# A hand-written order of 3920 steps is replaced by another, and two VectorE steps no longer wait for each other

## The chip, the cores and the metric

One core of a Trainium2 chip runs the program. The time is the device time of one execution in microseconds (us), the median of the runs; three runs of the kernel before took 1454.66 to 1455.35 us. Engines are named PE (TensorE), DVE (VectorE), ACT (ScalarE) and POOL (GpSimd) in the profile; SP issues transfers.

## What is computed

Three stages over 8192 tokens of 192 numbers, all in float32 from the outside:

```python
# 1: every token is a softmax-weighted sum of itself and the 6 tokens before it, 8 heads of 24
w = softmax(weight_gen, axis=-1)                      # (2, 4096, 8, 7)
out = einsum('bshk,bskhg->bshg', w, windows_of_7(x))  # x: (2, 4096, 192)
x = out.reshape(8192, 192)
# 2: a gated layer, 192 -> 1536 -> 192
x = (sigmoid(x @ w_gate) * (x @ w_val)) @ w_out
# 3: a rational layer, 192 -> 2048 -> 192
h = x @ w_in
P = a[0] + a[1]*h + a[2]*h**2 + a[3]*h**3
Q = 1 + abs(b[0])*abs(h) + abs(b[1])*h**2
return (P / (Q + 1e-6)) @ w_out2
```

## The kernel before

The tokens go through in blocks of 512 (the last two of 256), 17 in all. Matmuls of stages 1 and 2 run in a rounded float32 form; each operand is split into a high and a low part, so that a product takes five matmuls.

**The order.** Every piece of work is a *step* with a short name (`do_g`, `do_S`, ...). A step that is done hands the next one its data with `then`, into a queue of that name. The string ORDER (line 40) lists 3920 names, and `run(ORDER)` (line 713) calls them one after the other; each call takes the oldest work of its name. As every engine runs its instructions in the order in which they were issued, ORDER fixes the order on each engine and on each transfer queue. Semaphores do the rest: an instruction waits for its data and for its buffer. So what a step's place in ORDER decides is what stands before and behind it on its own engine.

**The steps**, by what they do for a block:
- Stage 1: X loads the next x (line 161), Na, Nb and Nc make the softmax weights, B multiplies a shifted x by one tap's weights on VectorE (line 397), J adds that product to the sum with an adding transfer that GpSimd issues (line 413). Six J belong to a block; after the last one Z copies the tail columns on ScalarE (line 422), T1 transposes on TensorE, C1 and L1 split the result into high and low.
- Stage 2, for each of 12 chunks: g and v are five matmuls each into the one PSUM bank `pg` and the one bank `pv`. S is the sigmoid on ScalarE (line 472), which frees `pg`; M multiplies on VectorE and frees `pv`; G rounds to the high part on ScalarE; L on VectorE or l on GpSimd subtracts for the low part (line 496: one function, two engines); O adds the chunk to the output with five matmuls. E, E1, E2, C2 and L2 split that output for stage 3.
- Stage 3, for each of 16 chunks: H is five matmuls into one of two banks `h` (line 555); A is three activations on ScalarE (line 562); V and W on VectorE finish the numerator's powers and free the bank. For each pair of chunks: Q adds the two parts of the denominator with an adding transfer that GpSimd issues (line 588), R takes the reciprocal square root on ScalarE, U squares it (line 598), T and Y multiply by it and D corrects it, all three on VectorE by way of the helper at line 585 (lines 603 to 615). P is a chunk's output matmuls, in full float32 (line 627); F copies the finished block out (line 636).
- The weights come in during the first blocks, by the steps K, Ka, Kd, Kh, Kl (VectorE) or kl (GpSimd), and Kc.

R and S use different activation tables of ScalarE, and Nb (exp) a third; a change from one to another puts a table load in between.

In the middle the list repeats itself every two blocks, and a pair of blocks has two stretches of the same kind: a last B, the J behind it, and Z, each followed by the S and g that come next.

Of the kernel before, what the change touches and what calls it, by code (L numbers as in the profile page):

```python
# [40 lines left out]
X K Na Z Na Ka T1 Kd C1 Ka L1 K Kh Ka kl g Ka Nb Kd v Nb Nc K Kh Ka Kl S B Nc B Kc Kd J B Kh K g Ka Kl S Kd Kc J B  # L41
Kh Kl K Kd g Ka Kd Kh Ka Kl J Kh K Kl B M Kd v G K S g B Kh l M v G S Kl K O Kd M l Kc v G Kh l O Kl J O K M G L g
Ka Kd v S Ka g O J Kc S B Kh Kl X Kd M g Kc G v S L J Kh g K Ka Kl M O Kd G v S Ka g Kd Z Kh T1 K l M C1 v L1 kl G O
S M g G B Kh v S l Kc Ka g Kl Ka B O K B M l v G S L J Ka g M Kd v S g K O M Kd S v G K Kh g O Kl K B G Kh L Ka l O
M Kc S v Kl J G Ka g Ka L M Kc O Kd S g G Ka v L Kh K O B M kl O G v S L J Kc g M Kd v G S Ka g O M l K S v G B E g
M l E1 v S Kh Kd g Ka E2 M kl K O C2 S L2 v G Kd g Kc L J O M H Kd G K S v L A g M J B v S V X Ka g W Kd Ka O Kd O K
G H G L l M O S J Kd g G A v L H M Q V S v A W O M Z V v G W Ka l T1 O M C1 L1 O G l g G B v S R L g M B H Na J U v
A T H Y O A Q D O G V E l W S V H W O B A M J g B v G V S l W R g M Q E1 v Kd G E2 H C2 U L J O L2 A T H Y P R D O A
V P W U Q V H S W P T A M g B v G V S l H W R M g J Y v G D A O L B H U Q V P S W T J O Nb M g Kd v G Nc A H P A l V
W P Y S Q H D O A V g W M H V G S W l v A g M B G v S V l X R g W J M O Q R v G H U L U P T A P Y D O R V H Z U W P  # L50
T A H Y Q O D A P V S W P V W g M T G v S R L g M Y T1 G v D O L C1 L1 P U B S H T H A M Y g G v D S A g V l W O Q M
S V g G W l H S B v A B J g M Q H V S W P A O V P G W E l v E1 R J E2 M g B C2 H R L2 O U v G T A H M l P U V J W S
P Q Y O F D g G T A H Y v S l V A g W D H R Q V P W M O A B P B J G V v U l W H R M T O A Y v G D H U V l P A W J T
P S Q V O W H Y g D A H M B G v S V l X A g W J M P S Q V R W g O P G U L v Z T H R M Y O U v D G A H T P l A V W P
Q Y S O D H V g W A M H Na G v V S l A W g M Q P S V R W O T1 G P B U L v T O C1 L1 P R M g Y G U H l v A D H T Q P
A V W O S V H W Y P A D g Q V H S W g M B G v S L J A g M B O S V P W G E L v E1 R E2 M J g B C2 H R L2 O U v G T A
H M l P U V J W S P Q Y O F D g G T A H Y v S l V A g W D H R Q V P W M O A B P B J G V v U l W H R M T O A Y v G D
H U V l P A W J T P S Q V O W H Y Nb g D A H Nc P A Q V O W R M P V W v B G H U L J X O T R H A Y P D A Q P V W P Z
V U W H S T H Y A g D P S M Q V G g A W l v O S M V G g W l v S R g M v G T1 R M l O U B v T O C1 L1 P G U l H S Y H
D A g M P T G S v A V l W g Q M V O S W g Y G H l S v A D g M V Q H S W P B A B J O V P G W E l v E1 R E2 M g C2 H B  # L60
J R O L2 U v G T A H M l P U V Q W S P J Y O F D g G T A H Y v S l V A g W D H R Q V P W M O A B P B J G V v U l W H
R M T O A Y v G D H U V l P A W J T P S Q V O W H Y g D A H M B G v S V l X A g W J M P S Q V R W g O P G U L v Z T
H R M Y O U v D G A H T P l A V W P Q Y S O D H V g W A M H Na G v V S l A W g M Q P S V R W O T1 G P B U L v T O C1
L1 P R M g Y G U H l v A D H T Q P A V W O S V H W Y P A D g Q V H S W g M B G v S L J A g M B O S V P W G E L v E1
R E2 M J g B C2 H R L2 O U v G T A H M l P U V J W S P Q Y O F D g G T A H Y v S l V A g W D H R Q V P W M O A B P B
J G V v U l W H R M T O A Y v G D H U V l P A W J T P S Q V O W H Y Nb g D A H Nc P A Q V O W R M P V W v B G H U L
J X O T R H A Y P D A Q P V W P Z V U W H S T H Y A g D P S M Q V G g A W l v O S M V G g W l v S R g M v G T1 R M l
O U B v T O C1 L1 P G U l H S Y H D A g M P T G S v A V l W g Q M V O S W g Y G H l S v A D g M V Q H S W P B A B J
O V P G W E l v E1 R E2 M g C2 H B J R O L2 U v G T A H M l P U V Q W S P J Y O F D g G T A H Y v S l V A g W D H R
Q V P W M O A B P B J G V v U l W H R M T O A Y v G D H U V l P A W J T P S Q V O W H Y g D A H M B G v S V l X A g  # L70
W J M P S Q V R W g O P G U L v Z T H R M Y O U v D G A H T P l A V W P Q Y S O D H V g W A M H Na G v V S l A W g M
Q P S V R W O T1 G P B U L v T O C1 L1 P R M g Y G U H l v A D H T Q P A V W O S V H W Y P A D g Q V H S W g M B G v
S L J A g M B O S V P W G E L v E1 R E2 M J g B C2 H R L2 O U v G T A H M l P U V J W S P Q Y O F D g G T A H Y v S
l V A g W D H R Q V P W M O A B P B J G V v U l W H R M T O A Y v G D H U V l P A W J T P S Q V O W H Y Nb g D A H
Nc P A Q V O W R M P V W v B G H U L J X O T R H A Y P D A Q P V W P Z V U W H S T H Y A g D P S M Q V G g A W l v O
S M V G g W l v S R g M v G T1 R M l O U B v T O C1 L1 P G U l H S Y H D A g M P T G S v A V l W g Q M V O S W g Y G
H l S v A D g M V Q H S W P B A B J O V P G W E l v E1 R E2 M g C2 H B J R O L2 U v G T A H M l P U V Q W S P J Y O
F D g G T A H Y v S l V A g W D H R Q V P W M O A B P B J G V v U l W H R M T O A Y v G D H U V l P A W J T P S Q V
O W H Y g D A H M B G v S V l X A g W J M P S Q V R W g O P G U L v Z T H R M Y O U v D G A H T P l A V W P Q Y S O
D H V g W A M H Na G v V S l A W g M Q P S V R W O T1 G P B U L v T O C1 L1 P R M g Y G U H l v A D H T Q P A V W O  # L80
S V H W Y P A D g Q V H S W g M B G v S L J A g M B O S V P W G E L v E1 R E2 M J g B C2 H R L2 O U v G T A H M l P
U V J W S P Q Y O F D g G T A H Y v S l V A g W D H R Q V P W M O A B P B J G V v U l W H R M T O A Y v G D H U V l
P A W J T P S Q V O W H Y Nb g D A H Nc P A Q V O W R M P V W v B G H U L J X O T R H A Y P D A Q P V W P Z V U W H
S T H Y A g D P S M Q V G g A W l v O S M V G g W l v S R g M v G T1 R M l O U B v T O C1 L1 P G U l H S Y H D A g M
P T G S v A V l W g Q M V O S W g Y G H l S v A D g M V Q H S W P B A B J O V P G W E l v E1 R E2 M g C2 H B J R O
L2 U v G T A H M l P U V Q W S P J Y O F D g G T A H Y v S l V A g W D H R Q V P W M O A B P B J G V v U l W H R M T
O A Y v G D H U V l P A W J T P S Q V O W H Y g D A H M B G v S V l X A g W J M P S Q V R W g O P G U L v Z T H R M
Y O U v D G A H T P l A V W P Q Y S O D H V g W A M H Na G v V S l A W g M Q P S V R W O T1 G P B U L v T O C1 L1 P
R M g Y G U H l v A D H T Q P A V W O S V H W Y P A D g Q V H S W g M B G v S L J A g M B O S V P W G E L v E1 R E2
M J g B C2 H R L2 O U v G T A H M l P U V J W S P Q Y O F D g G T A H Y v S l V A g W D H R Q V P W M O A B P B J G  # L90
V v U l W H R M T O A Y v G D H U V l P A W J T P S Q V O W H Y Nb g D A H Nc P A Q V O W R M P V W v B G H U L J X
O T R H A Y P D A Q P V W P Z V U W H S T H Y A g D P S M Q V G g A W l v O S M V G g W l v S R g M v G T1 R M l O U
B v T O C1 L1 P G U l H S Y H D A g M P T G S v A V l W g Q M V O S W g Y G H l S v A D g M V Q H S W P B A B J O V
P G W E l v E1 R E2 M g C2 H B J R O L2 U v G T A H M l P U V Q W S P J Y O F D g G T A H Y v S l V A g W D H R Q V
P W M O A B P B J G V v U l W H R M T O A Y v G D H U V l P A W J T P S Q V O W H Y g D A H M B G v S V l X A g W J
# [19 lines left out]
def tile_kernel(ctx: ExitStack, tc: tile.TileContext, x, wg, w_gate, w_val, w_out1, w_in, w_out2, ca, cb, out):  # L115
# [629 lines left out]
```

## Time and profile before

| | us |
|---|---|
| median of 3 runs | 1454.94 (1454.66 to 1455.35) |
| the profiled execution | 1458.93 |
| its span in the profile | 1457.2 |
| TensorE, VectorE, ScalarE, GpSimd busy | 1353.4, 1249.1, 1208.6, 436.3 |
| granted TensorE clock, mean | 0.98 |

The span is the profiled execution from its first to its last instruction. A granted clock of 1.00 is the full 2.4 GHz. Busy times are those in which an engine had an instruction running; a wait is idle time ahead of an instruction, put down to what ended it. Five of the pairs of blocks lie between the copies F that start at 261.08 and 1114.22 us.

### The profile page before, as it was taken

What the parts mean: (1) busy time and instruction counts of PE and PEld (TensorE: products, weight loads), DVE (VectorE), ACT (ScalarE), POOL (GpSimd) and SP (SyncE); (2) the same over time, 40 slices, a digit from 0 to 9 for tenths busy, and PEclk for the clock granted to TensorE, in tenths of its full rate; (3) what the DMA queues carried; (4) which work ended last, traced back from release to release, by engine and by line L of the source; (5) the groups of instructions that cost most, each with busy time, mean ns of one, the idle gap of its engine ahead of it and who ended that gap; (6) DMA issues with size and microseconds to landing.
All of it is one profiled execution on the core that took longest, in us unless ns stands there. A gap on an engine that the chain in (4) does not pass through costs nothing.

```text
span 1457.2 us, 18316 instructions
## 1 busy us (share of the span) xinstructions
PE 1353.4 (93%) x6630; PEld 1159.0 (80%) x6630; DVE 1249.1 (86%) x1547; ACT 1208.6 (83%) x1733; POOL 436.3 (30%) x394
## 2 busy tenths in 40 slices
PE   1589999999999999999899999999999999999877
PEld 0367788888888888888788888888888888999777
DVE  7888888889798897989889797989979788878987
ACT  2455898989898897989889898888988988889985
POOL 5223322423243232423234232432324333222110
PEclk9699999999999999999999999999999999999999
DMA  6776453534545353554525355453535434433442
GB/s 159 182 191 155 87 118 65 126 63 98 107 87 120 70 107 75 100 113 87 118 55 124 73 102 107 77 120 69 111 69 113 101 71 89 79 67 67 85 96 55
DMA packets 51227, 144.12 MB, mean 99 GB/s; under 512 B 6212, under 2 KB 16322, under 8 KB 51136
## 3 DMA queue, kind: packets, MB, share of 16 engines
q0 software_dynamic: 32256, 102.51, 37.9%
q1 hardware_dynamic: 18880, 40.44, 9.2%
q8 instruction: 52, 0.85, 0.2%
q14 instruction: 39, 0.32, 0.1%
HBM read 31.51 MB, written 6.29 MB: 26 GB/s over the span
## 4 chain that ended last, share of the span: by engine, by line
PE 43%; DVE 18%; ACT 14%; DMA 11%; issue 9%; POOL 4%; SPq 0%; POOLq 0%; DVEq 0%; ACTq 0%
PE acc L627 11%; DVE v L585 6%; DMA x<-pr 5%; DMA q<-r 4%; DVE v L576 3%; POOL gl L498 2%; ACT r L594 2%; DVE q L585 2%; DVE v L581 2%; PE h L292 2%; ACT r L599 2%; PE h L293 2%; PE pg L292 2%; PE h L296 2%; PE h L295 2%
## 5 line engine op out<-in xcount | busy, mean ns | idle before, releaser
L627 PE MATMUL acc<-wo,v 128*128 128x192 f32 x2048 | 375.2, 331 | 13.6 <-DVE v L585 13.6
L627 PEld LDWEIGHTS acc<-wo,v 128*128 128x128 f32 x2048 | 349.5, 194 | 30.7 <-DVE v L585 13.1
L498 POOL TENSOR_TENSOR gl<-g,gh 128x512 fp32r<-128x512 f32 x141 | 222.0, 1574 | 476.5 <-ACT gh L492 476.5
L567 ACT ACTIVATE v<-h,co 128x512 f32<-128x512 f32 x256 | 199.8, 780 | 49.0 <-PE h L296 48.4
L589 POOL DMA_DIRECT2D q<-r x128 | 118.6, 926 | 326.2 <-ACT r L569 280.3
L576 DVE TENSOR_TENSOR v<-v,h 128x512 f32<-128x512 f32 x256 | 174.7, 683 | 35.1 <-ACT r L569 34.1
L581 DVE SCALAR_TENSOR_TENSOR v<-v,co,h 128x512 f32<-128x512 f32 x256 | 191.5, 748 | 9.1
L585 DVE SCALAR_TENSOR_TENSOR q<-q,r 128x1024 f32<-128x1024 f32 x128 | 156.7, 1224 | 40.2 <-ACT r L599 40.2
L585 DVE SCALAR_TENSOR_TENSOR v<-v,co,r 128x1024 f32<-128x1024 f32 x128 | 180.8, 1413 | 0.0
L569 ACT ACTIVATE r<-h,co 128x512 f32<-128x512 f32 x256 | 178.3, 696 | 0.0
L486 DVE TENSOR_TENSOR g<-sg,pv 128x512 f32<-128x512 f32 x192 | 131.3, 684 | 53.5 <-PE pv L296 43.7
L568 ACT ACTIVATE q<-h,co 128x512 f32<-128x512 f32 x256 | 176.2, 688 | 0.4 <-DVE v L585 0.4
L585 DVE SCALAR_TENSOR_TENSOR v<-q,v 128x1024 f32<-128x1024 f32 x128 | 168.4, 1316 | 4.0
L594 ACT ACTIVATE r<-q,co 128x1024 f32<-128x1024 f32 x128 | 147.3, 1153 | 19.7 <-DMA q<-r 19.0
L492 ACT CAST gh<-g 128x512 fp32r<-128x512 f32 x192 | 118.6, 618 | 51.7 <-DVE g L486 38.2
L474 ACT ACTIVATE sg<-pg 128x512 f32<-128x512 f32 x192 | 115.6, 602 | 38.7 <-PE pg L296 29.6
L416 POOL DMA_DIRECT2D x<-pr x96 | 85.6, 892 | 171.8 <-DVE pr L280 94.8
L599 ACT ACTIVATE r<-r 128x1024 f32<-128x1024 f32 x128 | 135.5, 1062 | 0.3
L292 PE MATMUL h<-X2h,W0h 128*128 128x512 f32 (+1 forms) x272 | 111.0, 408 | 13.1 <-DVE v L581 12.8
L292 PE MATMUL pg<-X1h,W0h 128*128 128x512 f32 (+1 forms) x192 | 80.8, 421 | 26.6 <-ACT sg L474 26.6
L293 PE MATMUL h<-X2l,W0h 128*128 128x512 f32 (+1 forms) x272 | 103.2, 379 | 0.0
L295 PE MATMUL h<-X2h,WT 128*128 128x512 f32 (+1 forms) x272 | 102.9, 378 | 0.0
(135 smaller groups left out, 2819.0 us busy)
## 6 DMA issues: line engine op xcount, KB each, us to landing
q<-r POOLq DMA_DIRECT2D x128, 512.0 KB, 4.6
x<-pr POOLq DMA_DIRECT2D x84, 384.0 KB, 4.2
x<-in_x_dram SPq DMA_DIRECT2D x13, 960.0 KB, 5.8
out_dram<-o SPq DMA_DIRECT2D x15, 384.0 KB, 4.2
v<-in_moe_w_out_dram SPq DMA_DIRECT2D x14, 384.0 KB, 4.0
x<-in_x_dram SPq DMA_DIRECT2D x3, 768.0 KB, 4.7
WT<-r SPq DMA_DIRECT2D x36, 64.0 KB, 3.2
x<-pr POOLq DMA_DIRECT2D x12, 192.0 KB, 3.5
```

Of the source, the lines that this page charges most:

```text
L292: mm(d, W0h[:, w], h[:, 0, :], start=True, stop=False)
L293: mm(d, W0h[:, w], lo[:, 0, :], start=False, stop=False)
L498: eng.tensor_sub(gl, g1, gh.bitcast(F32))
L567: nc.scalar.activation(v[:, e, :], ph, AF.Identity, scale=a3, bias=a2)
L568: nc.scalar.activation(q[:, e, :], ph, AF.Square, scale=b1r)
L569: nc.scalar.activation(a[:, e, :], ph, AF.Abs, scale=b0)
L576: nc.vector.tensor_mul(v, v, ph)
L581: nc.vector.scalar_tensor_tensor(out=v, in0=v, scalar=a1, in1=ph, op0=ALU.add, op1=ALU.mult)
L585: nc.vector.scalar_tensor_tensor(out=out, in0=in0, scalar=scalar, in1=in1, op0=op0, op1=op1, reverse0=neg)
L594: nc.scalar.activation(r, q, AF.Abs_reciprocal_sqrt, scale=USC, bias=usb)
L599: nc.scalar.activation(r, r, AF.Square, scale=2.0 ** -20)
L627: mm(acc[:, s // 2, (s % 2) * D:(s % 2 + 1) * D], g[:, (e * jb + s) * P:(e * jb + s + 1) * P], wo2[:, c, :], start=(c == 0 and s % 2 == 0) ...
```

## The change

ORDER is replaced as a whole. Every step occurs as often as before, but for one kind of choice: of the 192 subtractions for the low part 96 run on VectorE (L) and 96 on GpSimd (l), where it was 51 and 141, and of the 16 subtractions for weights 15 run on VectorE (Kl) and one on GpSimd (kl), where it was 12 and 4. T and Y follow U independently now, and D follows when both are done. All functions but these stay as they are:

```diff
     @step
     def do_U(b, p, v, q, r):
         nc.scalar.activation(r, r, AF.Square, scale=2.0 ** -20)
-        then("T", b, p, v, q, r)
-
-    @step
-    def do_T(b, p, v, q, r):
+        then("T", b, p, v, q, r, both := [])
+        then("Y", b, p, v, q, r, both)
+
+    def second(both, *work):
+        both.append(1)
+        if len(both) == 2:
+            then(*work)
+
+    @step
+    def do_T(b, p, v, q, r, both):
         stt(q, q, EPS1, r, ALU.add, ALU.mult)
-        then("Y", b, p, v, q, r)
-
-    @step
-    def do_Y(b, p, v, q, r):
+        second(both, "D", b, p, v, q)
+
+    @step
+    def do_Y(b, p, v, q, r, both):
         stt(v, v, a0, r, ALU.add, ALU.mult)
-        then("D", b, p, v, q)
+        second(both, "D", b, p, v, q)
```

Of ORDER, the two stretches of a pair from the last B of a block to the g behind the next S (the first kind, then the second; the lists before and after go through the same work in different order, so the stretches do not match step by step):

```
before  B G H U L J X O T R H A Y P D A Q P V W P Z V U W H S T H Y A g
after   B P M J X R V g W H U O A Y v T H G R l V P W Z Q D A P O U V H W S Y H A M g
before  B G v S V l X A g W J M P S Q V R W g O P G U L v Z T H R M Y O U v D G A H T P l A V W P Q Y S O D H V g
after   B A P J X G V v R l W P M g U R H Y U O T v G D Z H A Na P L A Q V P W Y O S V H W g
```

## Rows read from the trace of the kernel before

**Rows 1.** The page's first part: busy time, share of the span, instructions of each engine.
```profile
PE 1353.4 (93%) x6630; PEld 1159.0 (80%) x6630; DVE 1249.1 (86%) x1547; ACT 1208.6 (83%) x1733; POOL 436.3 (30%) x394
```

**Rows 2.** Busy time by stretch: length; busy and count of each engine; granted clock, DMA share, GB/s.
```profile
26.50:160.00 133.50, 106.59 (x414) 80.18 (x415) 113.29 (x210) 75.04 (x147) 38.08 (x34) 0.90 0.65 166
...
261.08:1114.22 853.14, 830.15 (x3981) 711.63 (x3980) 735.45 (x856) 746.31 (x1041) 271.14 (x235) 0.99 0.47 95
...
1402.85:1457.20 54.35, 40.65 (x224) 38.10 (x222) 42.56 (x45) 35.03 (x48) 5.16 (x6) 0.87 0.35 73
```

**Rows 3.** TensorE's waits, 261 to 1114 us: total, times, longest.
```profile
PE pg L292 <- ACT sg L474: 16.2, 10, 3.6
PE h L292 <- DVE v L581: 6.8, 18, 0.8
```

**Rows 4.** ScalarE's waits for transfers in the same stretch.
```profile
ACT o L426 <- DMA x<-pr: 19.3, 10, 3.7
...
ACT r L594 <- DMA q<-r: 9.1, 7, 1.8
```

**Rows 5.** Timeline of ScalarE: start, length, instruction, idle time before it; Z and one R.
```profile
463.02 0.62 ACT L426 COPY o<-x 128x512 f32<-128x512 f32 x1 [0.92 <-DMA x<-pr]
465.49 1.15 ACT L594 ACTIVATE r<-q,co 128x1024 f32<-128x1024 f32 x1 [1.85 <-DMA q<-r]
...
723.99 0.62 ACT L426 COPY o<-x 128x512 f32<-128x512 f32 x1 [3.67 <-DMA x<-pr]
```

**Rows 6.** Timeline, 713 to 719 us: the last B, the x load, J and Q.
```profile
713.76 0.95 DVE L280 TENSOR_TENSOR pr<-x,wn 128x768 f32<-128x768 f32 x1
...
714.74 0.33 SPq L165 DMA_DIRECT2D x<-in_x_dram  x1
...
715.00 0.86 POOL L416 DMA_DIRECT2D x<-pr  x1 [3.98 <-DVE pr L280]
...
718.78 0.86 POOL L589 DMA_DIRECT2D q<-r  x1 [2.92 <-ACT r L569]
```

**Rows 7.** Timeline of TensorE, at 473 and from 722 us.
```profile
473.87 0.50 PE L292 MATMUL pg<-X1h,W0h 128*128 128x512 f32 x1 [0.81 <-ACT sg L474]
...
722.37 0.39 PE L296 MATMUL h<-X2l,WT 128*128 128x512 f32 x1
...
723.50 0.39 PE L296 MATMUL h<-X2l,WT 128*128 128x512 f32 x1
727.53 0.80 PE L292 MATMUL pg<-X1h,W0h 128*128 128x512 f32 x1 [3.64 <-ACT sg L474]
...
731.52 0.53 PE L292 MATMUL pg<-X1h,W0h 128*128 128x512 f32 x1
```

**Rows 8.** Busy time of one stretch, its granted clock third from the end.
```profile
727.50:731.00 3.50, 3.47 (x9) 2.99 (x10) 3.43 (x5) 2.73 (x5) 0.86 (x1) 0.51 0.00 0
```

**Rows 9.** The chain of waits at 268 us: start, length, the eight matmuls of one P.
```profile
268.52 1.30 PE acc L627 x8
```

**Rows 10.** Timeline of GpSimd at 457 us: a J and the Q behind it.
```profile
456.68 0.87 POOL L416 DMA_DIRECT2D x<-pr  x1
457.26 1.18 POOL L589 DMA_DIRECT2D q<-r  x1
```

**Rows 11.** Groups by line and form: busy us, mean ns; idle before.
```profile
L498 POOL TENSOR_TENSOR gl<-g,gh 128x512 fp32r<-128x512 f32 x141 | 222.0, 1574 | 476.5 <-ACT gh L492 476.5
...
L585 DVE SCALAR_TENSOR_TENSOR v<-v,co,r 128x1024 f32<-128x1024 f32 x128 | 180.8, 1413 | 0.0
...
L498 DVE TENSOR_TENSOR gl<-g,gh 128x512 fp32r<-128x512 f32 x51 | 35.1, 688 | 23.6 <-ACT gh L492 23.5
```

**Rows 12.** Line 585 alone, step Y: shortest, median, longest ns.
```profile
L585 DVE SCALAR_TENSOR_TENSOR v<-v,co,r x128: 1272/1279/2321, 161.6 to 1447.4; 128x1024 f32<-128x1024 f32 x128
```

**Rows 13.** VectorE's longest waits, 261 to 1114 us.
```profile
DVE q L585 <- ACT r L599: 33.6, 35, 3.5
```

**Rows 14.** Timeline of ScalarE around one table load.
```profile
710.99 0.71 ACT L569 ACTIVATE r<-h,co 128x512 f32<-128x512 f32 x1
711.72 1.28 ACT L594 ACT_TABLE_LOAD   x1
...
713.01 1.15 ACT L594 ACTIVATE r<-q,co 128x1024 f32<-128x1024 f32 x1
```

More of the change, by code (lines that the diff above doesn't have):

```diff
@@ L40 @@
 ORDER = """
[L41 to L95, printed above, removed]
@@ L96 @@
-M P S Q V R W g O P G U L v Z T H R M Y O U v D G A H T P l A V W P Q Y S O D H V g W A M H G V v S l W A g M Q P S
-V R W O T1 G P U L v T O C1 M L1 P R Y G g U l H S D v A T g M H S Q V g W A Y P D S O V H G W l v A g M V Q H S W P
-B A B B J O V P G W E l v E1 R E2 M g C2 H J R L2 O B U v G T A H M l P U V Q W S P J Y O F D g G T A H Y v S l V A
-g W D H R Q V P W M O A B B J P G V v U l W H R M T O A Y v J G D H U V l P A W Q T P S V O W H Y g D A H M G V v S
-l W A g M Q B P X S J V R W g O P G U L v R T H Z M U Y O A v D G H V S l W P Q T A g M P Y S g D O V S W H G L v A
@@ L101 @@
-H M V Q P A W O V P G W R l T1 v B B O C1 M J R L1 P B G U g L U T H Y v A D H J Q V P A W O T S H V W P A B M J g B
-Y G v S l V R g W Q D H M U O A B J P T v G V E l W H E1 R E2 Y P C2 A J D O B P U Q V W O F T S H L2 Y H A J D g M
-P S V G A W g l v S V Q g Z W R M T1 v G O M U l P G T R v L O Y C1 U P D S P L1 T g M H Y G S H l A g D A v V W O S
-V Q H W M g G A L H v S V A g W M H S V Q W P A O V P G W R l v g M R H U v A T H M U V Q P W A Y P S D H V v E W A
-g T H E1 S Q V R O W Y E2 O D C2 G P G L A P L2 l M O R V W v G U L H M U T H A Y O D Q P G A V l P W T H V O A W Y
@@ L106 @@
-H R Q D P A V O W U V H W P A T H Y R Q P D A P V W V F H W U H A T Y P R Q D A P V P W U V H W T H A Y P R Q D A V
-P W H U V W P A T H Y R Q D A V P W U V H W T A H Y P R Q D A V P W U V H W T E H A E1 P Y R Q D A V P W U V E2 P C2
-W L2 H T R H Y A D P A V Q W H U V W P A T H Y Q D R A V P W H U V W P A T H F V Q R W Y H A D A V P W H V Q R W P A
-H U V W A T H R V Q W U Y H U D T P A T P R V A W Y H U Q D V P A W T H V P A W Y H R Q D U V P A W T H V P A W Y F
-Q R D U V W T P Y P D R Y P U D P T P Y P D P P F
+X K Na Z Na Ka T1 Ka Kd C1 L1 Ka K Ka Kd Kh g v S Kl K Kd Ka Kh Nb Kl Kh Nc Nb K Kl Nc Kc B B Kc B J M Kd G Ka L Kh
@@ new lines @@
+K g Kl Ka v Kd S O J Ka g B K M S Kd G g v L S Kh K O Kh Kl Kl J B M Kd v G Kc B Kh K l M G Kl Ka O Ka L J Kc g Kd v
+S Kd Kh K g O S Ka Kl J B Ka g Kh Kl X M Kd v S G Kc g L J Kh Kl O M K Kd v S G Ka M l g G v L S Kd Z K Kh T1 Kl g
+C1 L1 O Kh Kl Ka O B Kc B M J B v S G K g L M Kd v S G Ka g O M l K S v G B Kh g l M v K S Kl J g M Kd v S Kc Ka g
+Ka O K O G B L J G Ka M l O S Kd v G Kh g O Ka Kl K Kh M l v S G Kl Kc g M l v S J B Kc g M Kd v S Ka g O Kd K O G L
+J G M E O K l E1 S v G B Kh E2 M l g X C2 L2 v kl S Ka g M J v Kd Kc S Ka g Kd O K Kd H G L O A Na K O M G V v S l W
@@ new lines @@
+G Z g L Ka M T1 Kd S v C1 L1 g Ka Nb M O B v G Nc S H H A L g M B v S Q V A J g W B O V O W G L H G M l v S A J g M
+v V Q S R W O B H Kd G O U L J g M G A L v Y O M V H G W E l O E1 A E2 T v C2 Q D G O R L2 l P V U W S O Y H T g D H
+S M B G v R L J g M B v G U P L Kd S O Y P A J M g T G v V S l A W g D H S Q V P W A M B H V J X O A W Kd H G v V A
+l W g M Q V H S W O A H G V P A l W v Q Z V P R M W g H U O R Y v G T U H l A O D O R Q V A P W Y P U V H W S T H A
+D g M P Y S Q G A v L V g W M P S V G W R v l T1 M T O C1 O D G U L1 l P R Y U g T H S D v A B H M g Q V G A W l P Y
@@ new lines @@
+H S V v A W g M T Q H S D O A V P W G V v E l W R P E1 M E2 g B C2 U J H L2 B R O Y A v T H G D U P A L Q J V P W O
+V F W S H Y H A M g B T J v G S l V A g M O Q D S P W G R L v V W P M U B g Y J H S T O A D v G V H l W g M A Q B P
+B J S P R V X W O H G U L v A Y g J M H R V Q W O U T P G Na A v D P S L V H Z W g M A Y O T S Q v G R l V H W D g A
+M P P U V W S O Y H T G v A l g M D Q H S V O A W P G V v R l W T1 M P B C1 L1 U O Y H G R L g A T v D H U Q V P A W
+Y P S V O W T H D g A M H B S Q v G V A L J g W M O S V P W G E L v E1 R E2 M P B C2 J g U L2 B H R Y O A T v G D H
@@ new lines @@
+U L Q J P A V W P Y O F V S W H T H A D g M O Q V S G W v A l g M V G P S L R W v B P M J B U g R Y H U T O A D v G
+H V S l W P J Y A g Q M P T S Nb D O H G Nc v A g L Q V O S W P M V G H W l v A B P M J X R V g W H U O A Y v T H G
+R l V P W Z Q D A P O U V H W S Y H A M g T v S Q D G g A L O M V S P W G R L v V W P M U T1 Y O C1 L1 P G R l H U T
+g A D v S H V Q W P B A M g Y O S V H W G L v A T g D Q H S M V O A W P B G V v E l W R P E1 J M E2 g B C2 U H L2 R
+Y O A T v J D H G U P L Q A V P W Y O F V S H W B H A M J g T v G D S A g L Q M O V S W P G V R l W v B P M U J B g
@@ new lines @@
+R Y H U T O A D v G V H S l W P J Y A g Q M T P S D O V H G W l v A g M V Q H S W O B A P J X G V v R l W P M g U R
+H Y U O T v G D Z H A Na P L A Q V P W Y O S V H W g M A T v D S Q H G L g A M V O W S P V G R W l v T1 M P C1 B L1
+U O Y H G R L g A T v D H U Q V P A W Y P S V O W T H D g A M H B S Q v G V A L J g W M O S V P W G E L v E1 R E2 M
+P B C2 J g U L2 B H R Y O A T v G D H U L Q J P A V W P Y O F V S W H T H A D g M O Q V S G W v A l g M V G P S L R
+W v B P M J B U g R Y H U T O A D v G H V S l W P J Y A g Q M P T S Nb D O H G Nc v A g L Q V O S W P M V G H W l v
@@ new lines @@
+A B P M J X R V g W H U O A Y v T H G R l V P W Z Q D A P O U V H W S Y H A M g T v S Q D G g A L O M V S P W G R L
+v V W P M U T1 Y O C1 L1 P G R l H U T g A D v S H V Q W P B A M g Y O S V H W G L v A T g D Q H S M V O A W P B G V
+v E l W R P E1 J M E2 g B C2 U H L2 R Y O A T v J D H G U P L Q A V P W Y O F V S H W B H A M J g T v G D S A g L Q
+M O V S W P G V R l W v B P M U J B g R Y H U T O A D v G V H S l W P J Y A g Q M T P S D O V H G W l v A g M V Q H
+S W O B A P J X G V v R l W P M g U R H Y U O T v G D Z H A Na P L A Q V P W Y O S V H W g M A T v D S Q H G L g A M
@@ new lines @@
+V O W S P V G R W l v T1 M P C1 B L1 U O Y H G R L g A T v D H U Q V P A W Y P S V O W T H D g A M H B S Q v G V A L
+J g W M O S V P W G E L v E1 R E2 M P B C2 J g U L2 B H R Y O A T v G D H U L Q J P A V W P Y O F V S W H T H A D g
+M O Q V S G W v A l g M V G P S L R W v B P M J B U g R Y H U T O A D v G H V S l W P J Y A g Q M P T S Nb D O H G
+Nc v A g L Q V O S W P M V G H W l v A B P M J X R V g W H U O A Y v T H G R l V P W Z Q D A P O U V H W S Y H A M g
+T v S Q D G g A L O M V S P W G R L v V W P M U T1 Y O C1 L1 P G R l H U T g A D v S H V Q W P B A M g Y O S V H W G
@@ new lines @@
+L v A T g D Q H S M V O A W P B G V v E l W R P E1 J M E2 g B C2 U H L2 R Y O A T v J D H G U P L Q A V P W Y O F V
+S H W B H A M J g T v G D S A g L Q M O V S W P G V R l W v B P M U J B g R Y H U T O A D v G V H S l W P J Y A g Q
+M T P S D O V H G W l v A g M V Q H S W O B A P J X G V v R l W P M g U R H Y U O T v G D Z H A Na P L A Q V P W Y O
+S V H W g M A T v D S Q H G L g A M V O W S P V G R W l v T1 M P C1 B L1 U O Y H G R L g A T v D H U Q V P A W Y P S
+V O W T H D g A M H B S Q v G V A L J g W M O S V P W G E L v E1 R E2 M P B C2 J g U L2 B H R Y O A T v G D H U L Q
@@ new lines @@
+J P A V W P Y O F V S W H T H A D g M O Q V S G W v A l g M V G P S L R W v B P M J B U g R Y H U T O A D v G H V S
+l W P J Y A g Q M P T S Nb D O H G Nc v A g L Q V O S W P M V G H W l v A B P M J X R V g W H U O A Y v T H G R l V
+P W Z Q D A P O U V H W S Y H A M g T v S Q D G g A L O M V S P W G R L v V W P M U T1 Y O C1 L1 P G R l H U T g A D
+v S H V Q W P B A M g Y O S V H W G L v A T g D Q H S M V O A W P B G V v E l W R P E1 J M E2 g B C2 U H L2 R Y O A
+T v J D H G U P L Q A V P W Y O F V S H W B H A M J g T v G D S A g L Q M O V S W P G V R l W v B P M U J B g R Y H
@@ new lines @@
+U T O A D v G V H S l W P J Y A g Q M T P S D O V H G W l v A g M V Q H S W O B A P J X G V v R l W P M g U R H Y U
+O T v G D Z H A Na P L A Q V P W Y O S V H W g M A T v D S Q H G L g A M V O W S P V G R W l v T1 M P C1 B L1 U O Y
+H G R L g A T v D H U Q V P A W Y P S V O W T H D g A M H B S Q v G V A L J g W M O S V P W G E L v E1 R E2 M P B C2
+J g U L2 B H R Y O A T v G D H U L Q J P A V W P Y O F V S W H T H A D g M O Q V S G W v A l g M V G P S L R W v B P
+M J B U g R Y H U T O A D v G H V S l W P J Y A g Q M P T S Nb D O H G Nc v A g L Q V O S W P M V G H W l v A B P M
@@ new lines @@
+J X R V g W H U O A Y v T H G R l V P W Z Q D A P O U V H W S Y H A M g T v S Q D G g A L O M V S P W G R L v V W P
+M U T1 Y O C1 L1 P G R l H U T g A D v S H V Q W P B A M g Y O S V H W G L v A T g D Q H S M V O A W P B G V v E l W
+R P E1 J M E2 g B C2 U H L2 R Y O A T v J D H G U P L Q A V P W Y O F V S H W B H A M J g T v G D S A g L Q M O V S
+W P G V R l W v B P M U J B g R Y H U T O A D v G V H S l W P J Y A g Q M T P S D O V H G W l v A g M V Q H S W O B
+A P J X G V v R l W P M g U R H Y U O T v G D Z H A L Y P A Q V P W T O S D H M g V G v W l S A g M H S V Q W O A P
@@ new lines @@
+G V v R l W T1 M P B C1 L1 U O Y H G R g L A T v D H U Q V P A W Y P S V O W T H D g A M H S V Q v G W A l g M O S V
+P W G E L v E1 R E2 M P B B J C2 g U L2 H R Y O A T v D G H U L Q J V P A W Y P V O F W S H T H D A g M B v G V S l
+W A g M J B O S Q V P G W R l v P M U g J Y H S T O A D v G V H l W g M A Q B P B J X S V P R W O H G U L v A Y J g
+M H R V Q W O U T P G D A v L P Y S V H W Z g M A T O D S Q v G R V l H W M g A P P U V W S O Y H T G v A l g M D Q
+H S V O A W P G V v R l W T1 M P B C1 B O U L1 J B H Y G R g L A T v D H U Q V J P A W B P Y S O V W H M T g G A l v
@@ new lines @@
+H S J D Q g M A V O W S B P G V E L v W R E1 J P M E2 B g C2 U L2 H R Y O A T v J D G H U L Q P A V W P B V O F W J
+S Y H T H A D g M O Q S V G v A W l g M V G P S W l Z R v T1 M P C1 U L1 O Y H G R L g T A v D H U Q V P W A Y P T S
+O D H M V g G A W l v H S V Q M g A W O S V P G W R l v P M U g R Y H U T v A D H Y Q P A V P W S V H W T H E A E1 g
+D O S Q M V O G A L v W E2 M g C2 G L2 O l V S W P G R L H v A P M U H V Q W R O Y H G T U P l A P D A O V W O R V Q
+H W U Y H T P A D P Y P A V P W R V Q H W F T U H A D Y P A V P W Q V H W R T H A D A V P W U H V Q W P A Y H T R D
@@ L111 @@
+A V P W U Q V H W R Y H A T P A D V P U Q W V H R W Y H A T P E D A E1 P V U Q W V R E2 P W C2 U H L2 Y H T A D Y P
+A V P W R V Q H W U T H A D Y P A V P W V Q H R W T H U D A Y P A V P W V Q H F W R T H A D A V P W H U V Q W P A Y
+H T R D A V P W U Q V H W R Y H A T P A D V P U Q W V R H W Y U H A T P D A V P W Q V R H W U Y H A T P D F A V W Y
+Q R V P W U T P D Y P T P D R U P Y P T D P P F
 """
```

## The prediction

> **What bounds the kernel now.** I read the page's busy times first. TensorE is busy for 93% of the span, VectorE for 86%, ScalarE for 83%, GpSimd for 30% [rows 1], so time is to be gained only where TensorE stands still. The table of stretches says where. In the head, from 26.5 to 160 us, TensorE is idle for 26.9 of 133.5 us and VectorE is busy for 113.3. In the periodic stretch, five pairs of blocks cut at the copies of finished blocks (line 636), TensorE is busy for 830.15 of 853.14 us: 170.6 us a pair, 4.6 of them idle. In the tail behind 1402.85 it is idle for 13.7 of 54.35 us [rows 2].
>
> The periodic stretch is the longest, so its waits come next. TensorE waits there for a sigmoid, S, ten times for 16.2 us, and for VectorE's release of a PSUM bank, W, 18 times for 6.8 us [rows 3]. ScalarE in turn waits for adding transfers: ten copies Z for a J transfer, 19.3 us, and seven steps R for a Q transfer, 9.1 us [rows 4]. ScalarE's queue is in order, so S stands behind Z and R, and these are one story told twice. Each pair has two kinds of place.
>
> First kind: the last product B of a block ends at 714.71; the load of the next x (960 KB) is issued at 714.74 and J at 715.00, both let go by that B, with a Q at 718.78 [rows 6]. J is not home until Z starts at 723.99, after a wait of 3.67 us [rows 5]. Copy, square, table load and sigmoid follow, and TensorE, whose five matmuls before took 1.13 us start to start, stands 3.64 us ahead of g. It then runs at half clock: g and a P take from 727.53 to 731.52 [rows 7], at a granted 0.51 [rows 8], the 1.2 GHz level where 2.4 went before. At full clock g is 1.13 and P 1.30 [rows 9], so 3.99 - 2.43 = 1.56 us more are lost. Second kind: a Q is issued right behind J, at 457.26 behind 456.68 [rows 10]; Z waits for 0.92 us and R, right behind it, for 1.85 [rows 5]; most is absorbed, and g at 473.87 waits for 0.81 [rows 7].
>
> **The change, part by part.** Both lists hold 3920 steps, and TensorE does the same work. Distances below are TensorE steps counted in the lists (g, v, O, H at 1.13 us, P at 1.30).
>
> *The Z places.* From that B to Z there are 3 x 1.13 + 3 x 1.30 = 7.3 us in the first kind before and 5 x 1.13 + 2 x 1.30 = 8.3 in the second. After, both have 8.3, and no Q stands between J and Z in either. Gain: TensorE's ten waits are 16.2 us; five of the second kind at 0.81 are 4.1, which leaves 2.4 for one of the first. With 0.1 for refilling and 1.56 of clock a pair loses 2.4 + 1.56 + 0.81 + 0.2 = 5.0 us. What remains after lies between nothing and two waits of the second kind (0.9 each, 1.8): B, the x load and J still start together, so some wait of Z stays. I take the middle, 0.9, since the distance is that of the second kind but its Q is gone. Gain 4.1 a pair, 20.5 in five. Such places also lie on either side of the stretch; I put them at 0 to 5 and count none.
>
> *Nothing between S and g.* In one pair 11 of 24 g follow the sigmoid that frees their bank with no TensorE step between, after it 2; of v behind M three, then one. The waits priced above hold these, so this is not counted again.
>
> *Subtractions moved from GpSimd.* L (VectorE) goes from 51 to 96, l (GpSimd) from 141 to 96, kl from 4 to 1. On GpSimd one costs 1574 ns, on VectorE 688 [rows 11]. VectorE gets 45 x 0.688 = 31.0 us, some 5.5 a pair. In return Y, 1413 ns on average [rows 11] at a median of 1279 [rows 12], loses part of its stretching, if that comes from GpSimd's subtractions: 128 x 0.134 = 17 us over 141 of them, 0.12 each, 5.5 us over 45. VectorE is busy for 147.1 us of a pair and goes to about 151.6 of some 166: still below TensorE. Behind an added L in its queue stand V and W, which free H's bank; the price is between nothing and 4.5 us a pair. As W already costs 6.8 us in five pairs [rows 3] and H's distances stay (none in two of 32, three before), I take 0.4 a pair, 2 us. On GpSimd's queue J and Q stand behind fewer l, each of which waits for its cast; SP's x load is bound to B, not to its place, so nothing is credited there.
>
> *T and Y freed of each other.* Before, T stands first behind U, after, mostly Y. VectorE waits there 35 times for 33.6 us [rows 13]. The first of the two keeps its distance of one step (9 of 16 in a pair in either list), so I take zero; the one that runs second covers D.
>
> *Table loads.* S and R now alternate more: 130 loads against 122 in the lists. A load takes 1.28 us, begins 0.02 us after the activation before it ends, and R starts 0.01 us after it [rows 14]. So 8 x 1.3 = 10.4 us on ScalarE, which is idle for 21 us of a pair; between 0 and 10.4, I take 1. The Trainium skill's page "ScalarE: Activation LUTs" (What ACT_TABLE_LOAD costs) states another 1.38 us of draining with each load, 2.66 in all, which speaks against this change: eight would be 21 us, and my term 2 in place of 1. The trace doesn't show that drain.
>
> *Head and tail.* Up to the first finished block VectorE gets one L and three more low parts of weights, about 4 us at 0.688 and more; VectorE is the bound there, so 0 to 4, taken as 2. In the tail TensorE waits for VectorE's last products; their work is the same, and I take nothing, within 4 us either way.
>
> Sum: -20.5 + 2 + 1 + 2 = -15.5 us. The profiled execution took 1458.93 us with a span of 1457.2, 4 us above the median of 1454.94; I set the difference against the median: 1439 us.
>
> **The rivals.**
> - *All waits of the periodic stretch go.* A pair's steps are 104 x 1.13 + 32 x 1.30 = 159.1 us, with transposes and folds at most 4.6: 163.7, or 6.9 less than now. Five pairs give 34.5 and the places beside them up to 5: 1415 to 1420. For it: nearly every zero distance is gone. Against it: J still starts with the x load.
> - *The transfers come as late as before.* If the x load sets when J lands, one us of distance moves little: Z keeps 2 to 3 us, TensorE's wait stays, and the costs of 5 us above stand against small gains: 1450 to 1460, about 1455. For it: J let go by B took 9 us in the row, with the x load beside it. [...]
> - *Slower: VectorE sets the pace.* Each added L delays W, and with it H. It decides once VectorE's 151.6 us and its needed waits fill a pair of 166, that is if over 14 of today's 23.5 us of idle time a pair are needed. Then 45 x (0.688 - 0.12) = 25.5 us come on top and the shorter wait of Z only moves to W: 1480. Against it: much of its waiting is only being early.
>
> **How the numbers follow.** Forecast 0.56, all waits gone 0.14, transfers as late 0.14, VectorE 0.16. About 0.2%, 3 us, is what a measurement here can tell from no change. Faster: 0.56 + 0.14 + 0.05 of the late transfers = 0.75; same 0.07; slower 0.02 + 0.16 = 0.18. The range takes in the bounds (0 to 5 of the places beside, 0 to 1.8 a pair at Z, 4 of head and tail), most of the case below and all of the late transfers short of their upper end: 1415 to 1458, which leaves out nearly all of the slow case and little else.
>
> **What would show it.** In the changed profile: the pairs at some 167 us; TensorE's wait for S in them from 16.2 to under 6 us and no half clock behind it; Z's wait for J halved; waits for W up by a few us; VectorE some 25 us busier, GpSimd 70 less; ScalarE with 65 and 58 loads. Z's waits unchanged would prove the second rival, and TensorE's waits for W above 20 us the slow one.

## The result and the profile after

The changed kernel takes 1417.43 us (four runs, 1416.54 to 1419.69) against 1454.8 of the kernel before in the same runs: a ratio of 0.9746, with a 95% interval of 0.9729 to 0.9763, so 37 us less where 15.5 were forecast. The direction and the largest term, the waits behind Z, held; the size did not.

The profiled execution took 1417.47 us with a span of 1415.7. The execution before that was profiled lay 4 us above its own median, so the two spans differ by 41.5 us, a few more than the runs. By the copies of finished blocks the span divides so:

| stretch | before | after | difference |
|---|---|---|---|
| start to the first finished block | 261.08 | 254.86 | -6.2 |
| first to eleventh (five pairs) | 853.14 | 825.11 | -28.0 |
| eleventh to the end | 342.98 | 335.73 | -7.3 |

The page's first part answers to [rows 1]:

```profile
PE 1337.3 (94%) x6630; PEld 1149.3 (81%) x6630; DVE 1250.3 (88%) x1598; ACT 1220.5 (86%) x1741; POOL 342.6 (24%) x343
```

TensorE has the same 6630 matmuls and is busy for 16 us less; the mean granted clock rose from 0.980 to 0.993, so fewer of them run at half clock. GpSimd lost 94 us, and VectorE, with 51 instructions more, is busy for only 1.2 us more. The table of stretches, columns as in [rows 2]:

```profile
26.50:160.00 133.50, 106.91 (x415) 80.44 (x414) 113.58 (x219) 78.79 (x153) 33.60 (x29) 0.94 0.67 169
160.00:254.86 94.86, 94.75 (x453) 80.62 (x452) 86.72 (x109) 87.04 (x124) 27.34 (x25) 1.00 0.46 89
254.86:1079.97 825.11, 820.01 (x3981) 705.72 (x3980) 739.92 (x896) 757.03 (x1048) 191.72 (x195) 1.00 0.49 99
```

The pairs went from 170.6 to 165.0 us, their idle time from 4.6 to 1.0, and the granted clock from 0.99 to 1.00. Between 160 us and the first finished block TensorE now stands still for 0.1 us; the row before for that stretch shows 4.1:

```profile
160.00:261.08 101.08, 96.96 (x461) 81.54 (x459) 89.29 (x113) 92.94 (x131) 29.53 (x29) 1.00 0.47 91
```

TensorE's waits in the five pairs, 255 to 1080 us, answer to [rows 3], ScalarE's for transfers to [rows 4]:

```profile
PE pg L292 <- ACT sg L474: 3.2, 4, 0.8
PE h L292 <- DVE v L581: 1.6, 2, 1.3
```
```profile
ACT o L426 <- DMA x<-pr: 8.7, 5, 2.9
```

S fell from 16.2 to 3.2 us, and W, which was to rise, from 6.8 to 1.6. Five copies Z still wait, those of every second block; R no longer does. Two lines of ScalarE's timeline and two of TensorE's show what is left:

```profile
374.85 0.62 ACT L426 COPY o<-x 128x512 f32<-128x512 f32 x1
622.12 0.62 ACT L426 COPY o<-x 128x512 f32<-128x512 f32 x1 [2.95 <-DMA x<-pr]
```
```profile
626.13 0.50 PE L292 MATMUL h<-X2h,W0h 128*128 128x512 f32 x1 [1.33 <-DVE v L581]
628.36 0.50 PE L292 MATMUL pg<-X1h,W0h 128*128 128x512 f32 x1 [0.78 <-ACT sg L474]
```

These two are what reaches TensorE here, and no half clock follows them (granted 1.00 from 626 to 634 us). The first is not the work of Z alone: VectorE stood for 2.05 us ahead of a softmax step (Na) that waited for its load, and for 0.43 us more for the activations behind Z. On VectorE and GpSimd instructions were stretched less than before (columns as in [rows 11]):

```profile
L585 DVE SCALAR_TENSOR_TENSOR v<-v,co,r 128x1024 f32<-128x1024 f32 x128 | 167.6, 1309 | 31.3 <-ACT r L599 31.3
L498 POOL TENSOR_TENSOR gl<-g,gh 128x512 fp32r<-128x512 f32 x96 | 129.6, 1350 | 308.3 <-ACT gh L492 300.4
```

Y takes 1309 ns in place of 1413, and a subtraction on GpSimd 1350 in place of 1574.

### The profile page after: what moved, and what is told of

Same layout as the page of the kernel before. It is cut to its first block, busy times and chain, and to the rows that moved or that the text cites. A ratio compares the mean times of both kernels' runs of the same rounds, so it can differ in the third digit from the quotient of the medians.

```text
span 1415.7 us, 18173 instructions
## 1 busy us (share of the span) xinstructions
PE 1337.3 (94%) x6630; PEld 1149.3 (81%) x6630; DVE 1250.3 (88%) x1598; ACT 1220.5 (86%) x1741; POOL 342.6 (24%) x343
## 4 chain that ended last, share of the span: by engine, by line
PE 73%; ACT 7%; issue 7%; DVE 6%; DMA 6%; POOL 1%; SPq 0%; POOLq 0%; DVEq 0%; ACTq 0%
PE acc L633 17%; DMA x<-pr 5%; PE h L292 3%; PE h L293 3%; PE h L295 3%; PE h L294 3%; PE h L296 3%; PE pg L292 3%; PE pv L292 3%; PE pg L293 3%; PE pg L294 3%; PE pg L296 3%; PE pg L295 3%; PE pv L293 3%; PE pv L296 3%
## 5 line engine op out<-in xcount | busy, mean ns | idle before, releaser
L633 PE MATMUL acc<-wo,v 128*128 128x192 f32 x2048 | 369.4, 328 | 16.1 <-DVE v L585 16.1
L633 PEld LDWEIGHTS acc<-wo,v 128*128 128x128 f32 x2048 | 342.1, 190 | 34.7 <-DVE v L585 17.9
L498 POOL TENSOR_TENSOR gl<-g,gh 128x512 fp32r<-128x512 f32 x96 | 129.6, 1350 | 308.3 <-ACT gh L492 300.4
L585 DVE SCALAR_TENSOR_TENSOR v<-v,co,r 128x1024 f32<-128x1024 f32 x128 | 167.6, 1309 | 31.3 <-ACT r L599 31.3
L585 DVE SCALAR_TENSOR_TENSOR v<-q,v 128x1024 f32<-128x1024 f32 x128 | 159.9, 1249 | 4.0
L492 ACT CAST gh<-g 128x512 fp32r<-128x512 f32 x192 | 119.8, 624 | 32.4 <-PE acc L513 15.4
L294 PE MATMUL h<-X2h,W0l 128*128 128x512 f32 (+1 forms) x272 | 102.6, 377 | 0.0
```

The costliest lines, as they stand in the source:

```text
L294: mm(d, W0l[:, w], h[:, 0, :], start=False, stop=False)
L585: nc.vector.scalar_tensor_tensor(out=out, in0=in0, scalar=scalar, in1=in1, op0=op0, op1=op1, reverse0=neg)
L633: mm(acc[:, s // 2, (s % 2) * D:(s % 2 + 1) * D], g[:, (e * jb + s) * P:(e * jb + s + 1) * P], wo2[:, c, :], start=(c == 0 and s % 2 == 0) ...
```

## The experiments

**Z behind S, in the list before.** The theory was that a transfer which is late stands at the head of ScalarE's in-order queue and holds up the sigmoid behind it. One step is moved, five times.

```diff
-P Z V U W H S T H
+P V U W H S Z T H
```

> The kernel before, with one step moved at five places: in the first kind of place the copy Z, which waits for the last J transfer of a block, stands behind the square U and the sigmoid S instead of ahead of them. Theory 1 (a late transfer at the head of ScalarE's queue holds up the sigmoid, and with it TensorE and its clock): the five TensorE waits of 2 to 3.6 us and the half clock behind them go, 4.1 us each, so 1434 to 1440 us, and no stretch at 0.5 clock is left at these places. Rival (the lateness lies in the list as a whole, and the next step behind Z is held up instead): 1450 to 1455 us, with the wait showing at H or g a few us later.

Measured: 1435.96 us, ratio 0.988 (0.9858 to 0.9902), 17.5 us less by the ratio, 19.6 by the medians. The copies that open and close the five pairs, TensorE's waits between them, and the stretch:

```profile
258.45 0.80 ACT L635 COPY o<-acc 128x768 f32<-128x768 f32 x1
...
1091.65 0.80 ACT L635 COPY o<-acc 128x768 f32<-128x768 f32 x1
```
```profile
PE h L291 <- DVE v L580: 7.5, 19, 1.1
PE pg L291 <- ACT sg L473: 4.6, 6, 0.8
```
```profile
261.08:1092.00 830.92, 818.70 (x3972) 703.18 (x3971) 732.61 (x854) 742.28 (x1037) 269.93 (x235) 1.00 0.48 97
```

A pair takes 166.6 us, 4.0 less than 170.6, where 4.1 were expected; the wait for S falls from 16.2 to 4.6 us and the clock is 1.00. The wait of Z itself became shorter too (8.1 us in place of 19.3), and nothing came back at the H behind it. The chain is seen in the kernel before, too: its five long waits for S in the pairs, 1.96, 2.28, 3.64, 2.16 and 2.15 us, are each 0.02 to 0.04 us shorter than the wait of the Z ahead of them, and the granted clock falls to 0.5 behind every one. So half of the whole gain is five moves of one step, and the first kind of place is shown.

**The moved subtractions alone, in either list.** The k-th subtraction for a low part is put on the engine that it has in the other kernel; nothing else changes.

```diff
-B P B J G V v U l W H R M T O A Y v G D
+B P B J G V v U L W H R M T O A Y v G D
```

(One of 96 such places; 69 go to VectorE, 24 to GpSimd, and 3 of the weights' to VectorE. In the list after it is the reverse.)

> The kernel before in its own order, but the k-th subtraction for a low part runs on the engine that it has in the kernel after: 96 on VectorE and 96 on GpSimd in place of 51 and 141, and 15 and 1 of the weights' in place of 12 and 4. Theory 1 (the places of Z carry the gain, the moved subtractions cost VectorE time): 1455 to 1465 us, TensorE's wait for W longer than before. Theory 2 (the slow subtractions on GpSimd hold up J and Q behind them, and stretch VectorE's instructions): 1435 to 1450 us, with Z's waits for J shorter.

> The kernel after in its own order, but the k-th subtraction for a low part runs on the engine that it has in the kernel before (51 on VectorE, 141 on GpSimd; weights 12 and 4). Theory 1 (order alone): 1414 to 1422 us. Theory 2 (the moved subtractions carry a part of the gain): 1425 to 1440 us, with J and Q issued later and Z and R waiting for them.

Measured: the list before with the new engines 1460.66 us, ratio 1.0044 (1.0025 to 1.0062), slower by 6 us; the list after with the old engines 1418.42 us, ratio 0.9751 (0.9735 to 0.9767), the same as the kernel after. TensorE's waits from 258 to 1080 us, first of the one, then of the other:

```profile
PE pg L291 <- ACT sg L473: 15.9, 10, 3.3
PE h L291 <- DVE v L580: 7.4, 18, 1.0
```
```profile
PE pg L291 <- ACT sg L473: 3.2, 4, 0.8
PE h L291 <- DVE v L580: 1.3, 2, 1.1
```

The wait for W follows the list (6.8 and 7.4 in the old, 1.6 and 1.3 in the new), not the 45 subtractions. The loss shows in the head, and W's wait is hardly longer: the first block is finished at 264.21 us, where five profiles with the old list up to there show 258.45 to 261.08; the five pairs take 853.7 us, against 853.1. What the subtractions do to VectorE is seen in the first kernel's Y:

```profile
L584 DVE SCALAR_TENSOR_TENSOR v<-v,co,r 128x1024 f32<-128x1024 f32 x128 | 171.9, 1343 | 0.0
```

1413 - 1343 = 70 ns times 128 is 9 us for 45 subtractions less on GpSimd, 0.2 each, against the 0.12 of the forecast. But Y alone does not tell it. In the new list Y changes by only 10 ns (1319 to 1309) and T by 97. T, Y and D together go from 505.9 to 488.3 us in the old list and from 498.7 to 486.1 in the new: 0.39 and 0.28 us for each subtraction. So VectorE is busy for only 2.7 us more in the old list and 15.4 in the new, where some 25 were expected. The moved subtractions carry none of the gain.

**T always first, in the list after.** Y stood first in all 128 places; the two names are exchanged.

```diff
-F V S W H T H A D g M O Q V S G W
+F V S W H Y H A D g M O Q V S G W
```

> The kernel after, but of each T and Y the earlier place is always T's and the later Y's, as in the kernel before. Theory 1: no difference, 1415 to 1420 us, VectorE's wait behind U as long as with Y first. Rival (the freedom of T and Y is worth something): 1425 us or more.

Measured: 1417.87 us, ratio 0.975 (0.9729 to 0.9771). VectorE's wait behind U, in the kernel after and in this one, 258 to 1080 us:

```profile
DVE v L585 <- ACT r L599: 24.7, 26, 2.1
```
```profile
DVE q L584 <- ACT r L598: 24.5, 26, 2.1
```

It does not matter which of the two stands first, so their freedom carries none of the gain; VectorE's wait there fell from 33.6 [rows 13] to 24.7 us with the list.

**R later as well, in the list before.** On top of Z behind S, R and U of the second kind of place go behind one round of A and the cast G, at six places.

```diff
-Z T H R M Y O U v D G A H T
+Z T H M Y O v D G A R U H T
```

> The kernel before with Z behind S in the first kind of place (as in z_behind_s, 1436.0 us), and in the second kind, at six places, R and U behind the next round of activations A and the cast G, so that R no longer stands at the head of ScalarE's queue while its Q, issued right behind a J, is on its way. Theory 1 (the two transfer waits, 2.8 us together, make TensorE's wait of 0.81 us for S there): 1429 to 1433 us, R's wait gone and TensorE's waits for S near zero. Rival (the rest of the gain of the new list lies elsewhere): 1434 to 1438 us.

Measured: 1440.53 us, ratio 0.9896 (0.9881 to 0.991): no faster than z_behind_s (the intervals overlap, the median is 4.6 us above it) and outside of both expectations. TensorE's only wait row and ScalarE's wait of R, 255 to 1080 us:

```profile
PE h L291 <- DVE v L580: 14.7, 20, 1.3
```
```profile
ACT r L593 <- DMA q<-r: 1.1, 2, 0.8
```

R's wait is gone (9.2 us in z_behind_s) and so is every wait for S, as the theory said, but the wait for W doubled, from 7.5 to 14.7. T stands behind U on VectorE and V and W behind T: the wait moved to VectorE's queue, as at one of five such places in the pairs:

```profile
465.01 1.23 DVE L584 SCALAR_TENSOR_TENSOR q<-q,r 128x1024 f32<-128x1024 f32 x1 [3.22 <-ACT r L598]
```
```profile
467.67 0.50 PE L291 MATMUL h<-X2h,W0h 128*128 128x512 f32 x1 [0.85 <-DVE v L580]
...
471.50 0.51 PE L291 MATMUL h<-X2h,W0h 128*128 128x512 f32 x1 [1.25 <-DVE v L580]
```

This move of R did not mend the second kind of place; the new list also puts Q elsewhere.

**The same edit in the list after.** Z goes behind the next S at five places, and Na, which waits for its load at the head of VectorE's queue, behind the next W at four of them. (At those four Z waits, for 1.56 to 2.95 us; at the fifth, behind the pairs, it does not. The pairs' remaining wait of Z, 0.73 us, is left as it is.)

```diff
-D Z H A Na P L A Q V P W Y O S V H W g
+D H A P L A Q V P W Y O S Z V H W Na g
```

> The kernel after with the same edit where its own Z still waits, 1.6 to 2.95 us in every second block: Z stands behind the next S (five places), and the softmax's Na, which waits for its load, behind the next W (four places). Theory 1: TensorE's remaining waits in the pairs, 4.8 us in five, go: 1411 to 1415 us, faster than either kernel. Rival (the rest is hidden or comes back elsewhere): 1416 to 1419 us.

Measured: 1411.31 us, ratio 0.9698 (0.9684 to 0.9712), faster than both kernels. The copies at either end of the five pairs, and the stretch:

```profile
255.92 0.80 ACT L641 COPY o<-acc 128x768 f32<-128x768 f32 x1 [0.17 <-PE acc L632]
...
1074.57 0.80 ACT L641 COPY o<-acc 128x768 f32<-128x768 f32 x1 [0.17 <-PE acc L632]
```
```profile
260.00:1085.00 825.00, 824.68 (x4010) 710.89 (x4010) 746.09 (x905) 763.64 (x1057) 194.65 (x198) 1.00 0.50 99
```

A pair takes 163.7 us and TensorE stands still for 0.3 of 825 us. That is the 163.7 which the prediction's first rival worked out as a pair without waits. Which of the two moves gives how much was not taken apart.

**Which stretch of the list is worth what.** Three lists have the new order in one stretch and the old in the rest, leaving out what is done; a fourth is the new list behind the old head.

> The list after up to the first finished block (638 steps), then the list before with the steps already done left out; T and Y free as in the kernel after. The first finished block came 6.2 us earlier in the profile of after, with 1 us less of TensorE work done. Theory 1 (the head is worth 5 us by itself, mostly TensorE's clock): 1447 to 1452 us. Rival (VectorE's extra 4 us of low parts cost what the clock gives; the earlier copy came of the places of Z ahead of it): 1454 to 1459 us.

> The list before up to the first finished block, the list after from there to the eleventh, the list before for the rest. In the profiles the ten blocks of the middle took 853.1 us before and 825.1 after. Theory 1 (the places of Z carry some 20 us of it, the shorter waits for W and S the other 8): 1425 to 1430 us, and together with head_new and tail_new the whole 37 us. Rival (the parts lean on each other, and the middle without its own head gives only the 20 us of z_behind_s): 1434 to 1438 us.

> The list before up to the eleventh finished block (3016 steps), then the list after with the steps already done left out. From there to the end the kernel after took 7.3 us less. Theory 1 (the end's own order is worth it): 1446 to 1450 us. Rival (VectorE and ScalarE come into the end less far behind TensorE, and the end's own order is worth little): 1453 to 1457 us.

> The list before up to the first finished block, then the list after to the end. Theory 1 (parts add up; head_new alone was worth 3 us by the runs, 6 by the profile): 1419 to 1424 us. Rival (the head's gain in the profile is one run's clock and not the list's): 1416 to 1419 us.

| new list in | us | ratio (95% interval) | gain by the ratio |
|---|---|---|---|
| the head (head_new) | 1452.36 | 0.9978 (0.9963 to 0.9992) | 3.2 |
| the ten blocks (middle_new) | 1435.08 | 0.9862 (0.9834 to 0.989) | 20.1 |
| the end (tail_new) | 1449.62 | 0.9963 (0.9949 to 0.9977) | 5.4 |
| all but the head (head_old) | 1424.89 | 0.9789 (0.9762 to 0.9816) | 30.7 |
| everything (the kernel after) | 1417.43 | 0.9746 (0.9729 to 0.9763) | 37.0 |

The three parts give 28.7 us, not 37. Seams take much of the rest, places where one list passes into the other and the steps that one had done early leave the other in another mix for a block or two. In head_new the block behind the seam takes 87.4 us:

```profile
254.92 0.80 ACT L641 COPY o<-acc 128x768 f32<-128x768 f32 x1 [0.16 <-PE acc L632]
342.31 0.80 ACT L641 COPY o<-acc 128x768 f32<-128x768 f32 x1
```

In the kernel before it took 84.0 (261.08 to 345.11). In middle_new the block behind the second seam takes 86.1 (1086.25 to 1172.39), 3.4 more than before, and in tail_new the two blocks behind it 165.8, where they took 162.1:

```profile
1109.58 0.80 ACT L641 COPY o<-acc 128x768 f32<-128x768 f32 x1
...
1275.39 0.80 ACT L641 COPY o<-acc 128x768 f32<-128x768 f32 x1 [0.66 <-PE acc L632]
```

With 3.4, 3.4 and 3.7 us for the seams, an estimate from one profile each, the parts make 6.6 + 23.5 + 9.1 = 39 us, which is the whole within the intervals. Of the four expectations only that for tail_new was met. head_new and head_old lie 0.4 and 0.9 us above the upper ends of their first theories. middle_new missed its 1425 to 1430 and has the time of its rival, by which the parts lean on each other. The seam, which was not thought of, explains 3.4 us of the miss; against the rival speaks that the ten blocks themselves took 825.9 us, as in the kernel after.

## Why the prediction was wrong in size

By the steps of its sum, with what stands in their place:

- **The Z places, -4.1 a pair: right.** z_behind_s took 4.0 a pair from the old list by the first kind alone. In the kernel after S still costs 3.2 us in five pairs, 0.64 a pair, and 0.9 was left for it. With the prediction's own 5.0 a pair as the loss before, that is 4.3, 21 us in five pairs in place of 20.5. The reason given for what remains, that J still starts with the x load, is not enough. J is issued 0.3 us behind that load in both kinds of place. In one kind Z starts 7.4 to 7.5 us after J without a wait. Where Z waits, it starts 9.0 to 10.4 us after J at four of the five places, and there a load of softmax weights is issued as well, 0.1 us behind J.
- **W, +2 us: wrong, and in sign.** The prediction took the waits for H's bank for a matter of VectorE's load, since H's zero distances in the list stayed much alike (two in place of three a pair), and let 45 more subtractions lengthen them. They went from 6.8 to 1.6 us; with the prediction's own 0.1 for refilling, 16 waits fewer make it some 7 us. The pair of exchanged engines shows that the load has little to do with it: 0.6 us. That the order does it is shown, and the trace of the kernel before says where. Of its 18 waits 15 are at the three places of a pair where no TensorE step stands between W and H. There VectorE has Y and D (five times) or Y, D, T and Y (ten times) to do between the last V and W and these, without a pause; the ten cost 4.3 of the 6.8 us. One of these, from T on:

```profile
432.15 1.22 DVE L585 SCALAR_TENSOR_TENSOR q<-q,r 128x1024 f32<-128x1024 f32 x1
433.29 2.32 DVE L585 SCALAR_TENSOR_TENSOR v<-v,co,r 128x1024 f32<-128x1024 f32 x1
435.53 0.68 DVE L576 TENSOR_TENSOR v<-v,h 128x512 f32<-128x512 f32 x1
436.24 0.75 DVE L581 SCALAR_TENSOR_TENSOR v<-v,co,h 128x512 f32<-128x512 f32 x1
```
```profile
437.04 0.50 PE L292 MATMUL h<-X2h,W0h 128*128 128x512 f32 x1 [0.41 <-DVE v L581]
```

  The new list has nine such places in the five pairs, and TensorE waits at none: VectorE has one step there, Y or D, between the last V and W and these. The two waits for W that are left stand behind the softmax step that waits for its load. So the prediction's count of zero distances was not enough: in the traces, what stands ahead of V and W on VectorE tells the places that cost something from those that do not. No run moves these steps alone.
- **Table loads, +1: no trace of them.** ScalarE is busy for 11.9 us more, about the 10.4 of eight loads, and idle time paid for it.
- **Head, +2: wrong in the sum.** The cost is there in the old order, as before_moved_subs shows with its first block at 264.21 us. In the new order it is gone: 255.88 us with the old engines (after_old_subs), 254.86 with the new. And there is a gain, at the places "on either side" of the pairs, put at 0 to 5 and counted as none: between 160 us and the first finished block 4 us of idle time went, two waits for S behind an R whose Q was late (2.5 us) and one for W (1.4). The head is worth 3.2 us as measured. The 6.2 of the table are too many, as the profile of the kernel before is the latest of the five with the old head.
- **Tail, 0 within 4: wrong.** It was worth 5.4 us as measured, 7.3 in the profile. Behind the eleventh finished block TensorE's waits for W and S fell from 6.2 to 0.8 us, its waits for VectorE's last products, the ones that the prediction looked at, rose from 13.6 to 16.1, and it was busy for 4.3 us less. The half clock is the smaller part of it. The stretch between the fifteenth and the sixteenth copy, in the kernel before, in the old order at a better clock (before_moved_subs) and in the kernel after:

```profile
1402.85:1437.29 34.44, 28.06 (x160) 26.08 (x158) 30.05 (x34) 29.76 (x43) 4.30 (x5) 0.85 0.43 88
```
```profile
1405.39:1438.41 33.02, 25.49 (x160) 23.12 (x158) 30.07 (x34) 29.66 (x42) 4.29 (x5) 0.95 0.45 92
```
```profile
1366.18:1395.14 28.96, 24.79 (x164) 22.20 (x163) 27.81 (x32) 27.59 (x38) 3.44 (x4) 1.00 0.52 105
```

  The old order at 0.95 still takes 4.1 us more than the new. Which moves give the tail its time is not shown.

So the step that failed is the setting of three terms by how much work an engine has, where the order of the steps decided. W, the head and the tail were to cost 4 us together; W gave some 7, the head 3.2 and the tail 5.4. The pairs (28.0 us in the profile, some 21 of S and 7 of W) and the two ends make 36.6 of the 37. Of the rivals the first, no waits left in the pairs, names the measured time (1415 to 1420), but for another reason: the pairs stopped at 165.0 us, and the head and tail made up for it. The second is refuted by the shorter waits, the third by the exchanged engines. The page "ScalarE: Activation LUTs" of the Trainium skill (What ACT_TABLE_LOAD costs) gives 2.66 us for each change of table, by which, an estimate, the eight loads would cost 21 us on ScalarE. The trace has the load alone: ScalarE is 11.9 us busier, and it is idle for only 1.0 us in all ahead of the 58 loads that come with an R, whose work starts 0.01 us behind the load [rows 14].

## What to carry to other kernels

A step that waits for a transfer should not stand, on its in-order engine, ahead of a step for which the bounding engine waits: moving one copy behind the sigmoid at five places gave 1.2%, and the same move in the new list, together with one on VectorE, another 0.4%. Price such a wait with the clock that falls behind it, and look for the same pattern in the head and the tail before setting them to zero. Ask the same of the step that frees a buffer: what stands ahead of it on its own engine counts, and not only its distance from the step that waits. A wait that is cured by delaying a step can come back where that step's result is at the head of another queue, as R's did at W.

## What was not expected of the hardware

The clock in the head differs between executions of the same instructions, and here it costs nothing that can be seen. Up to the first finished block tail_new and head_old issue the same list as the kernel before; from 26.5 to 160 us the granted clock was 0.90 in the first, as in [rows 2], and 0.97 in the second:

```profile
26.50:160.00 133.50, 107.30 (x419) 81.29 (x420) 114.40 (x211) 76.16 (x149) 38.60 (x34) 0.90 0.65 166
```
```profile
26.50:160.00 133.50, 106.85 (x417) 80.67 (x416) 113.16 (x209) 75.98 (x148) 38.32 (x34) 0.97 0.64 164
```

Their first blocks were finished at 258.52 and 258.56 us. The kernel before and middle_new, also at 0.90, were later, at 261.08 and 260.31, so the difference of 2.6 us between executions of one list has another cause, which stays open.

An adding transfer of 384 KB, issued at 611.75 us beside the loads of the next x and of softmax weights, let Z start only at 622.12: 10.4 us, where 4.0 is the median from issue to landing.
